# Low words and passes of weight chunks 1 and 2 moved ahead of the first main product of a linear-attention and two-layer expert kernel

## The chip, the cores and the metric

One core of a Trainium2 chip runs the whole program. The metric is the time of one execution on the device in microseconds (us), the median of several runs. The core has five engines, each with an instruction queue of its own that it works through in order: TensorE (PE in the profile, its weight loads PEld), VectorE (DVE), ScalarE (ACT), GpSimd (POOL) and SyncE (SP), which here issues the direct DMAs. Engines wait for each other through semaphores. TensorE writes into PSUM, the others read it from there.

## The reference

Three stages run one behind the other. The first is a recurrent attention over 4 batches, 8 heads, 768 steps and a head size of 48; the second a feed-forward net with a leaky rectifier; the third a choice of one of 8 experts for each of the 3072 tokens.

```python
for t in range(S):                                  # stage 1
    cur = np.einsum('bhd,bhe->bhde', u[None] * kt, vt)
    y[:, :, t] = np.einsum('bhd,bhde->bhe', rt, state + cur)
    state = wt[:, :, :, None] * state + np.einsum('bhd,bhe->bhde', kt, vt)
h = x @ w_in                                        # stage 2: 384 -> 2048 -> 384
g = np.maximum(h, 0.0) + alpha * np.minimum(h, 0.0)
x = g @ w_out
logits = xn @ en.T / tau                            # stage 3: xn, en are normed rows
expert_idx = np.argmax(logits, axis=1)
out[mask] = gate_w[mask, None] * (np.maximum(x[mask] @ w1[e], 0.0) @ w2[e])
```

The weights w_in and w_out come as 64-bit floats (the setup draws them so), and the kernel gets them as pairs of 32-bit words.

## The kernel before

**Tiles and blocks.** The 3072 tokens are 24 tiles of 128 steps (tile n is chunk n // 4 of batch n % 4), taken in 8 blocks of three. For each block the feed-forward net runs as 16 groups f of 128 hidden columns: `l1(j, f)` (L400) makes nine matmuls of 128 x 384 (high and low parts of x and of the weights in three combinations), ScalarE copies the result times alpha, VectorE takes the minimum with it, ScalarE makes the high part gh, and `l1_lo` (L421) the low part gl on VectorE. `l2(j, f)` (L425) adds nine matmuls to the block's output two groups later. In the text below the first, second and third group are f = 0, 1 and 2 of block 0.

**Weight chunks.** w_in and w_out are each cut into eight pieces of two groups. Chunk c is piece c // 2 of w_in where c is even and of w_out where it is odd. A chunk is loaded into one of four stage buffers (`load_stage`, L181) and turned into floats by `conv(q, ...)` (L190) in four steps: q = 0 scales the low words (ScalarE, L196), q = 1 merges them with the high words in two passes (VectorE, L198 and L199), q = 2 writes the rounded high part, win0h or wout0h for the first half (ScalarE, L210), q = 3 the low part (VectorE, L212). Behind q = 3 of chunk c the load of chunk c + 4 is issued on SP's queue. The chunks 0 to 3 are loaded at the start. For a w_out piece, `wprime_a` (L223) transposes it on TensorE (six transposes, two copies on ScalarE) and `wprime_b` (L237) multiplies it with the normed expert rows enT (48 small products), so that the router's logits come out of l2 as eight more columns.

**Attention pieces.** ATT (L395) lists ten pieces of a tile: 0 and 1 are scans and products on VectorE, 6 the product with r and 7 the diagonal, 2 the transposes of k into Kt, 3 the scores (TensorE, two A copies on ScalarE, masks on GpSimd), 9 the state products with their copies, 4 the output y, 5 the transposes of y into xh and xl, 8 the square of w - 0.95 on ScalarE, from which the kernel later learns whether its scaling was safe. Small PSUM results of all these pieces take turns in three buffers, those of l1 in two.

**The order.** It is written out by hand. The string PLAN (L78) is run first, item by item; each engine gets its instructions in that order. `aq.n` is piece q of tile n, `cq.c` step q of chunk c, `wk` is k warm-up matmuls, `lk.f` is l1 or l2 of group f of block 0, `pq.g` wprime_a or wprime_b of piece g, and `s` norms the expert rows (two small VectorE operations, a ScalarE product, three transposes, a copy into enT). Then a loop over steps T runs the rest (L945): for T = 0, wprime_b of piece 0, the low words of chunk 4, the passes of chunk 3, the scan of tile 3, the low part of chunk 2, gl of the first group, the high part of chunk 3; each T goes one chunk further, and group T stands at step T. What PLAN has run already the loop leaves out (`run`, L856). So the third group's l1 comes at T = 2, behind wprime_b of piece 1.

**Loads.** Tiles 0 and 1 have the two load buffers, tile 2 lies in a part of the buffer att2 (L146), from which a later weight tile is made. Tile 3's load is issued behind piece 9 of tile 0, tile 4's behind piece 9 of tile 1, those of later tiles behind piece 4. The expert rows `en` (L119) share a buffer with the wprime copies `wt` and later rows, so `s` had to come ahead of wprime_a.

Of the kernel before, what the change touches and what calls it, by code (L numbers as in the profile page):

```python
# [8 lines left out]
F32 = mybir.dt.float32  # L9
# [9 lines left out]
DM = H * D  # L19
# [3 lines left out]
NTILE = B * NCH  # L23
# [4 lines left out]
NE = 8  # L28
# [11 lines left out]
LD = LN + 3 * DM + LW  # L40
# [34 lines left out]
LAGS = [0, 1, 4, 4, 6, 7, 2]  # L75

LOADS = [(0, "w"), (0, "rk"), "id", "v", (0, "n"), "e", (1, "w"), (1, "rk"), (1, "n"), (2, "w"), (2, "rk"), (2, "n"), 0, 1, 2, 3, "u"]
PLAN = "a0.0 a1.0 a8.0 a2.0 w6 a6.0 a3.0 a7.0 w8 a0.1 a1.1 a6.1 a4.0 a3.1 a9.0 a2.1 c0.0 a7.1 w8 a0.2 a1.2 a6.2 c1.0 a4.1 w8 a3.2 a7.2 a5.0 c2.0 w6 a4.2 a5.1 a5.2 c3.0 l1.0 a8.1 a9.1 a2.2 a9.2 a8.2 c0.1 c1.1 l1.1 s c2.1 c0.2 p0.0 c3.1 c1.2 c2.2 c0.3"  # L78

AT1 = [0, 4, 8]  # L80
AT = {2: [-1, 6], 3: [-4, 1, 7]}
# [12 lines left out]
def tile_main(ctx, tc, keep, x2d, tbl, att, w_in, w_out, alpha, u_row, u_col, emb, tau, w1, w2, cst, out):  # L94
# [11 lines left out]
    rp = ctx.enter_context(tc.tile_pool(name="rows", bufs=1))  # L106
# [9 lines left out]
    u_bd = cp.tile([128, HP, 2], F32, name="u_bd")  # L116
    al_sb = cp.tile([128, KF], F32, name="al_sb")
    tau_sb = cp.tile([128, 1], F32, name="tau_sb")
    en = rp.tile([NE, DM], F32, tag="rows", name="en")  # L119
    enT = cp.tile([128, KD, NE], F32, name="enT")  # L120
    wmid = cp.tile([128, 1], F32, name="wmid")
    dev = cp.tile([128, NTILE], F32, name="dev")
# [21 lines left out]


    att2 = big.tile([128, KF // 2 * XW], F32, tag="W", name="att2")  # L146
    win = [[big.tile([128, KD, DFF // 2], F32R, tag="W", name=f"win{i}{q}") for q in "hl"] for i in range(2)]
    wout = []

# [7 lines left out]
    def load_att(n, part=None):  # L157
        if n not in ld_t:
            if n == 2:
                ld_t[n] = att2[:, 0:LD]  # L160
            else:
                ld_t[n] = ldp.tile([128, LD], F32, tag="ld", name="ld")
        m = LN + 2 * DM if n in ND else LN
        for s in {None: [slice(0, LN), slice(m, LD)] if n in ND else [slice(0, LD)], "w": [slice(LD - LW, LD)], "rk": [slice(0, LN)], "n": [slice(m, LD - LW)]}[part]:
            SP.dma_start(out=ld_t[n][:, s], in_=att[n][:, s])
# [15 lines left out]
    def load_stage(kind, g):  # L181
        t = sgp.tile([128, GF * DM, 2], I32, tag="sg", name="stg")
        if kind == "in":
            for k in range(KD):
                SP.dma_start(out=t[:, k * GF * 128:(k + 1) * GF * 128, :], in_=w_in[:, k, 2 * g * GF * 128:2 * (g + 1) * GF * 128])
        else:
            SP.dma_start(out=t, in_=w_out[:, g * GF:(g + 1) * GF, :])
        stage[kind, g] = t

    def conv(q, kind, g):  # L190

        t = stage[kind, g]
        lw, hw = t[:, :, 0], t[:, :, 1]
        lf = lw.bitcast(F32)
        if q == 0:
            ACT.activation(out=lf, in_=lw.bitcast(U32), func=AF.Copy, scale=-0.936 * 2.0 ** -51, bias=-2.0)  # L196
        elif q == 1:
            DVE.scalar_tensor_tensor(out=lw, in0=hw, scalar=3, in1=lw, op0=ALU.logical_shift_left, op1=ALU.bitwise_or)  # L198
            DVE.scalar_tensor_tensor(out=lw, in0=hw, scalar=0x3FFFFFFF, in1=lw, op0=ALU.bitwise_or, op1=ALU.bitwise_and)  # L199
        else:  # L200
            h, g0 = divmod(g, NG // 2)
            if kind == "in":
                hi, lo = (w[:, :, g0 * GW:(g0 + 1) * GW] for w in win[h])
            else:
                if h == len(wout):
                    wout_half()
                hi, lo = (w[:, g0 * GF:(g0 + 1) * GF, 0:DM] for w in wout[h])
            f3 = lf.rearrange("p (a b) -> p a b", a=(KD if kind == "in" else GF))
            if q == 2:
                ACT.activation(out=hi, in_=f3, func=AF.Copy, scale=-1.0)  # L210
            else:
                DVE.scalar_tensor_tensor(out=lo, in0=f3, scalar=-1.0, in1=hi.bitcast(F32), op0=ALU.mult, op1=ALU.subtract)  # L212
                del stage[kind, g]
# [175 lines left out]
    def warm(n):  # L389

        for _ in range(n):
            t = ps_h.tile([128, 3, 128], F32, tag="h", name="idle")
            PE.matmul(out=t, lhsT=oneb, rhs=oneb.rearrange("p (o t) -> p o t", o=1).to_broadcast([128, 3, 128]), start=True, stop=True)
# [406 lines left out]
    if True:  # L800
# [46 lines left out]
        sched = {}  # L847
        for n in range(NTILE):
            j = max(q for q in range(NB) if B0[q] <= n)
            t0 = START[n] if j == 0 else 16 * (j - 1) + (AT1 if j < 3 else AT[BLK[j]])[n - B0[j]]  # L850
            for q, d in enumerate(LAGS0 if j == 0 else LAGS1 if j == 1 else LAGS):
                sched.setdefault(t0 + d, []).append((q, n))

        ran = set()

        def run(kind, *a):  # L856
            if (kind, *a) in ran:
                return
            if kind != "w":
                ran.add((kind, *a))  # L860
            if kind == "a":
                q, n = a
                ATT[q](n)
                m = n + 3 if n < 2 else n + 2
                if q == (9 if n < 3 else 4) and n != 2 and m < NTILE:
                    load_att(m)
            elif kind == "c":
                q, c = a
                conv(q, ("in", "out")[c % 2], c // 2)
                if q == 3 and c + NSG < 2 * NG:  # L870
                    load_stage(("in", "out")[(c + NSG) % 2], (c + NSG) // 2)
            elif kind == "w":
                warm(*a)
            elif kind == "l":
                (l1, l2)[a[0] - 1](0, a[1])
            elif kind == "p":
                (wprime_a, wprime_b)[a[0]](a[1])
            else:
                DVE.tensor_scalar(out=en2, in0=en2, scalar1=1e-6, scalar2=None, op0=ALU.add)
                DVE.reciprocal(out=en2, in_=en2)  # L880
                ACT.activation(out=en, in_=en, func=AF.Copy, scale=en2)
                ep = ps_a.tile([128, KD, NE], F32, tag="a", name="ep")
                for k in range(KD):
                    PE.transpose(ep[:, k, :], en[:, k * 128:(k + 1) * 128], ident[0:NE, 0:NE])
                ACT.activation(out=enT, in_=ep, func=AF.Copy)

        def pieces(T, qs):
            for q, n in sched.get(T, []):
                if q in qs:
                    run("a", q, n)  # L890
                    if q == 6:
                        run("a", 7, n)

        def convs(T, late):
            for q, i in CONV[late]:
                c = T + OFF - i
                if 0 <= c < 2 * NG:
                    run("c", q, c)
# [43 lines left out]

        for t in PLAN.split():
            run(t[0], *(int(i) for i in t[1:].split(".") if i))
        for T in range(16 * NB + 2):  # L945
            j, f = divmod(T, 16)
            for i, d in enumerate(WPD):
                c = T + OFF - d
                if c % 2 and 0 <= c < 2 * NG:
                    run("p", i, c // 2)  # L950
            convs(T, 0)
            pieces(T, (2, 3, 4, 5))
            if 0 <= T and j < NB:
                run('l', 1, f) if j == 0 else l1(j, f)
            if T == 16 * (NB - 1):
                xg.extend(atp.tile([128, 2, ROW], F32, tag=t, name="xg") for t in ("st", "st", "at"))
                for t in xg:
                    POOL.memset(t, 0.0)
            if T >= 2:
                run('l', 2, T - 2) if T < 18 else l2((T - 2) // 16, (T - 2) % 16)  # L960
                if (T - 2) % 16 == 15:
                    o_evac((T - 2) // 16)
                    q = (T - 2) // 16
                    bg.append(chain(route(q), *((early_table(), early_loads()) if q == NB - 2 else (last_table(),) if q == NB - 1 else ())))
            if T >= 0:
                pieces(T, (0, 1, 6))
                convs(T, 2)
                if (j, f) in m_t:
                    l1_lo(j, f)
                convs(T, 1)  # L970
            step(STEP7 if j >= NB - 1 else 1)
            if T == 32:
                zero = sgp.tile([128, DM], F32, tag="sg", name="zero")
                POOL.memset(zero, 0.0)
            if 32 <= T < 32 + NTILE:
                SP.dma_start(out=out[(T - 32) * CH:(T - 31) * CH, :], in_=zero)
            for fn, i, at in EARLY:
                if T - 16 * NB == at:
                    (split, x_T)[fn](0, i)
# [31 lines left out]
        n = len(STEPS)  # L1011
# [318 lines left out]
```

## Time and profile before

| | us |
|---|---|
| median of 3 runs | 835.43 |
| lowest, highest run | 833.98, 836.77 |
| the profiled execution | 834.44 |
| its span, first to last instruction | 832.4 |
| TensorE busy | 796.8 (96% of the span) |
| VectorE busy | 585.0 (70%) |
| ScalarE busy | 436.9 (52%) |
| GpSimd busy | 297.2 (36%) |

The busy shares are means over stages with different limits. In the first 60 us attention of the first tiles, the loads and the turning of weights go on side by side, and TensorE is kept from falling silent by warm-up matmuls; behind that come the eight blocks, and behind them the experts. In the rows below, one line of a timeline gives the start in us, the time in us, the engine, the line of the kernel, the operation, what is written from what, the shape, the number of merged instructions, and in brackets the idle time before it with what ended it. One line of a window gives its start and end, its length, the busy time (and number of instructions) of PE, PEld, DVE, ACT and POOL, the granted clock of TensorE as a share of 2.4 GHz, the busy share of the DMA engines and GB/s. A line of waits says who waited for what: us in total, how often, the longest.

### The profile page before, as it was taken

To read this page: it belongs to the slowest core of one execution; us is meant where nothing else is said; L and a number is where in the kernel's file an instruction comes from. 1 tells how busy PE (TensorE), PEld (TensorE's weight loads), DVE (VectorE), ACT (ScalarE), POOL (GpSimd) and SP (SyncE) were. 2 spreads that over 40 slices of the span, in tenths; PEclk is the share of its full clock that TensorE was granted. 3 is DMA by queue.
4 is the path that set the end of the run, shared out by engine and by line. 5 is a ranking of instruction groups with operands and counts; after the bars stand their busy time and mean duration, and the time that the engine had idled before them with its cause. 6 is when DMAs were issued, how large, how long until landed. Compare 5 with 4: busy or idle time off the path is not lost. (4 is left out here: it accounts for less than half of the span.)

```text
span 832.4 us, 16488 instructions
## 1 busy us (share of the span) xinstructions
PE 796.8 (96%) x6464; PEld 758.3 (91%) x6464; DVE 585.0 (70%) x1229; ACT 436.9 (52%) x861; POOL 297.2 (36%) x365
## 2 busy tenths in 40 slices
PE   9669999999999999999999999997899999999996
PEld 5459989999999999999999999896889999999996
DVE  7478875886776676776777774646987776768662
ACT  6466664444444444544534443435556676767662
POOL 2001011343224224213214312154456777767731
PEclk9859999999999999999999999999999999999999
DMA  9434521123334323113113101046666877686750
GB/s 323 153 115 136 179 105 68 68 77 106 116 124 143 116 77 96 68 67 97 68 68 96 68 1 31 30 148 211 129 234 202 298 250 265 212 294 210 261 177 32
DMA packets 31623, 114.86 MB, mean 138 GB/s; under 512 B 5756, under 2 KB 13148, under 8 KB 29232
## 3 DMA queue, kind: packets, MB, share of 16 engines
q0 software_dynamic: 13952, 59.86, 22.1%
q1 hardware_dynamic: 17584, 53.85, 19.3%
q8 instruction: 53, 0.87, 0.5%
q14 instruction: 34, 0.28, 0.2%
HBM read 99.36 MB, written 15.51 MB: 138 GB/s over the span
## 5 line engine op out<-in xcount | busy, mean ns | idle before, releaser
L413 ACT ACTIVATE m<-h_ps,al_sb 128x384 f32<-128x384 f32 x128 | 74.1, 579 | 130.7 <-PE h_ps L409 123.6
L414 DVE TENSOR_TENSOR m<-h_ps,m 128x384 f32<-128x384 f32 x128 | 71.0, 555 | 98.6 <-ACT m L413 97.5
L417 ACT ACTIVATE gh<-m 128x384 fp32r<-128x384 f32 x128 | 67.2, 525 | 120.1 <-DVE m L414 116.8
L423 DVE TENSOR_TENSOR gl<-m,gh 128x384 fp32r<-128x384 f32 x128 | 80.3, 627 | 35.0 <-ACT gh L417 33.7
L337 POOL TENSOR_SCALAR_AFFINE_SELECT A<-A 128x512 f32<-128x512 f32 x48 | 29.8, 645 | 183.5 <-ACT A L336 183.5
L686 POOL DMA_INDIRECT raw<-in_w,wix x64 | 67.4, 1054 | 50.3 <-DVE w0l L698 23.4
L728 PE MATMUL h_ps<-yh,w0h 128*128 128x256 f32 x264 | 77.1, 292 | 3.7 <-DVE g2l L733 3.6
L728 PE MATMUL h_ps<-yl,w0h 128*128 128x256 f32 x264 | 74.7, 283 | 0.9 <-DVE yl L719 0.9
L728 PE MATMUL h_ps<-yh,w0l 128*128 128x256 f32 x264 | 74.3, 281 | 0.0
L698 DVE TENSOR_TENSOR w1l<-raw,w1h 128x768 fp32r<-128x768 f32 x64 | 60.6, 953 | 18.4 <-ACT w1h L697 12.6
L409 PE MATMUL h_ps<-xh,win0h 128*128 128x384 f32 x192 | 70.8, 369 | 2.1 <-DVE m L414 1.5
L698 DVE TENSOR_TENSOR w0l<-raw,w0h 128x768 fp32r<-128x768 f32 x64 | 60.8, 958 | 12.5 <-ACT w0h L697 11.6
L409 PE MATMUL h_ps<-xh,win1h 128*128 128x384 f32 x192 | 68.9, 359 | 0.5 <-DVE m L414 0.5
L409 PE MATMUL h_ps<-xh,win0l 128*128 128x384 f32 x192 | 66.8, 348 | 0.5 <-DVE win0l L212 0.4
L409 PE MATMUL h_ps<-xl,win0h 128*128 128x384 f32 x192 | 66.8, 348 | 0.1
L433 PE MATMUL o_ps<-wout1h,gl 128*128 128x392 f32 x192 | 65.4, 341 | 1.0 <-issue 1.0
L433 PE MATMUL o_ps<-wout0l,gh 128*128 128x392 f32 x192 | 65.5, 341 | 0.0
L433 PE MATMUL o_ps<-wout0h,gh 128*128 128x392 f32 x192 | 65.5, 341 | 0.0
L433 PE MATMUL o_ps<-wout0h,gl 128*128 128x392 f32 x192 | 65.5, 341 | 0.0
L433 PE MATMUL o_ps<-wout1h,gh 128*128 128x392 f32 x192 | 65.3, 340 | 0.1
L409 PE MATMUL h_ps<-xl,win1h 128*128 128x384 f32 x192 | 65.4, 341 | 0.0
L409 PE MATMUL h_ps<-xh,win1l 128*128 128x384 f32 x192 | 65.3, 340 | 0.0
(282 smaller groups left out, 2265.2 us busy)
## 6 DMA issues: line engine op xcount, KB each, us to landing
ld<-in_att SPq DMA_DIRECT2D x18, 1348.5 KB, 5.7
stg<-in_w_in SPq DMA_DIRECT2D x24, 256.0 KB, 3.1
stg<-in_w_out SPq DMA_DIRECT2D x8, 768.0 KB, 4.2
x2d<-rows SPq DMA_DIRECT2D x24, 194.0 KB, 7.9
out<-zero SPq DMA_DIRECT2D x24, 192.0 KB, 7.1
ld<-in_att SPq DMA_DIRECT2D x5, 512.0 KB
ld<-in_att SPq DMA_DIRECT2D x3, 452.5 KB, 5.2
raw<-in_w,wix POOLq DMA_INDIRECT x64
```

The costliest lines, as they stand in the source:

```text
L337: POOL.affine_select(out=h, in_=h, pattern=[[0, HP], [1, CH]], compare_op=ALU.is_gt, fill=0.0, base=0, channel_multiplier=-1)
L409: PE.matmul(out=h, lhsT=w[:, k, :], rhs=x[:, k, :], start=(n == 0), stop=(n == 3 * KD - 1))
L413: ACT.activation(out=m, in_=h, func=AF.Copy, scale=al_sb[:, f:f + 1])
L414: DVE.tensor_tensor(out=m, in0=h, in1=m, op=ALU.min)
L417: ACT.activation(out=gh, in_=m, func=AF.Copy)
L423: DVE.tensor_tensor(out=gl, in0=m_t.pop((j, f)), in1=gh.bitcast(F32), op=ALU.subtract)
L433: PE.matmul(out=o_t[j][i], lhsT=g[:, s], rhs=w, start=(f == 0 and n == 0), stop=(f == KF - 1 and n == 2))
L686: POOL.indirect_dma_start(out=t, out_offset=None, in_=src, in_offset=idx(wix[:, h, COL[s]:COL[s] + 1]))
L698: DVE.tensor_tensor(out=lo, in0=a, in1=hi.bitcast(F32), op=ALU.subtract)
L728: PE.matmul(out=h, lhsT=w[:, k, :], rhs=x[:, k, :], start=(n == 0), stop=(n == 3 * KD - 1))
```

## The change

PLAN gets another order; the rest are edits that make it possible.

- Piece 9 of tile 1 (state products and copies) goes from behind the first group to before the second row of warm-up matmuls; the low words of chunks 1 and 2 go to before tile 2's second scan; the passes of chunk 1 go to before tile 2's diagonal.
- Piece 5 of tile 1 goes ahead of the high part of chunk 0, and two warm-up matmuls are left out there. wprime_a of piece 0, the high part of chunk 1 and the passes of chunk 2 go ahead of the first group.
- Between the first and the second group come the low part of chunk 1 and the high part of chunk 2. Behind the second group come the low words of chunk 3, the low part of chunk 2, `s` and wprime_b of piece 0, and only then the square of tile 1, the transposes of k of tile 2 and its state products. The square of tile 2 goes to step T = 1 of the loop.
- `en` moves into a strip of att2 that tile 2 doesn't use, since wprime_a now comes ahead of `s`.
- The load of tile 4 is issued when pieces 4, 8 and 9 of tile 1 have all been run, which is now behind its square.

```diff
-PLAN = "a0.0 a1.0 a8.0 a2.0 w6 a6.0 a3.0 a7.0 w8 a0.1 a1.1 a6.1 a4.0 a3.1 a9.0 a2.1 c0.0 a7.1 w8 a0.2 a1.2 a6.2 c1.0 a4.1 w8 a3.2 a7.2 a5.0 c2.0 w6 a4.2 a5.1 a5.2 c3.0 l1.0 a8.1 a9.1 a2.2 a9.2 a8.2 c0.1 c1.1 l1.1 s c2.1 c0.2 p0.0 c3.1 c1.2 c2.2 c0.3"
+PLAN = "a0.0 a1.0 a8.0 a2.0 w6 a6.0 a3.0 a7.0 w8 a0.1 a1.1 a6.1 a4.0 a3.1 a9.0 a2.1 c0.0 a7.1 a9.1 w8 a0.2 c0.1 c0.2 a1.2 a6.2 c1.0 a4.1 w8 a3.2 c1.1 a7.2 a5.0 a5.1 c2.0 w4 a4.2 p0.0 c3.0 a5.2 c2.1 c1.2 l1.0 c3.1 c2.2 l1.1 c0.3 c3.2 s p1.0 a8.1 a2.2 a9.2"
...
-    en = rp.tile([NE, DM], F32, tag="rows", name="en")
...
     att2 = big.tile([128, KF // 2 * XW], F32, tag="W", name="att2")
+    en = att2[0:NE, LD:LD + DM]
...
+        sched[1].append((8, 2))
...
-                if q == (9 if n < 3 else 4) and n != 2 and m < NTILE:
+                if q in (4, 8, 9) and n != 2 and m < NTILE and (n > 2 or {("a", i, n) for i in (4, 8, 9)} <= ran):
                     load_att(m)
...
-                pieces(T, (0, 1, 6))
+                pieces(T, (0, 1, 6, 8))
```

## Rows read from the trace of the kernel before

**Rows 1.** The page's head: span and number of instructions.

```profile
span 832.4 us, 16488 instructions
```

**Rows 2.** Ten-microsecond windows: length, busy (count) per engine, clock, DMA share, GB/s.

```profile
20.00:30.00 10.00, 9.08 (x113) 6.34 (x113) 7.12 (x11) 4.82 (x13) 1.22 (x2) 1.00 0.53 170
30.00:40.00 10.00, 6.05 (x53) 4.80 (x52) 2.34 (x4) 5.78 (x13) 0.00 (x0) 0.84 0.56 177
40.00:50.00 10.00, 2.86 (x57) 2.34 (x57) 5.77 (x9) 6.31 (x12) 0.67 (x1) 0.50 0.24 81
50.00:60.00 10.00, 8.69 (x80) 7.70 (x80) 9.83 (x15) 5.05 (x10) 0.22 (x1) 0.64 0.33 88
```

**Rows 3.** Two long windows.

```profile
15.72:60.75 45.03, 30.71 (x348) 24.04 (x345) 29.89 (x42) 26.31 (x58) 3.33 (x6) 0.77 0.48 156
60.76:82.55 21.79, 21.59 (x256) 20.41 (x256) 19.61 (x28) 14.92 (x31) 2.71 (x5) 0.92 0.45 141
```

**Rows 4.** Timeline of VectorE, 30 to 62 us.

```profile
38.70 0.96 DVE L198 SCALAR_TENSOR_TENSOR stg<-stg 128x768 int32<-128x768 int32 x1 [5.42 <-ACT stg L196]
...
54.38 0.95 DVE L198 SCALAR_TENSOR_TENSOR stg<-stg 128x768 int32<-128x768 int32 x1
...
60.75 0.56 DVE L414 TENSOR_TENSOR m<-h_ps,m 128x384 f32<-128x384 f32 x1
```

**Rows 5.** ScalarE groups, 15.72 to 60.75: count, busy us, mean ns, idle before.

```profile
L196 ACT ACTIVATE stg<-stg 128x768 f32<-128x768 uint32 x7 | 6.3, 898 | 0.0
...
L210 ACT ACTIVATE wout0h<-stg 128x768 fp32r<-128x768 f32 x2 | 1.8, 912 | 0.9 <-DVE stg L199 0.9
...
L278 ACT ACTIVATE att<-att,wmid 128x512 f32<-128x512 f32 x1 | 0.7, 722 | 0.0
...
L234 ACT ACTIVATE wt<-wt_ps 128x512 f32<-128x512 f32 x2 | 1.2, 583 | 0.3 <-PE wt_ps L232 0.3
...
L235 ACT ACTIVATE wt<-wt_ps 128x256 f32<-128x256 f32 x2 | 0.7, 372 | 0.0
```

**Rows 6.** Timeline of ScalarE, 16 to 58 us.

```profile
19.44 1.91 ACT L307 ACTIVATE dv<-ld,dg 128x48 f32<-128x48 f32 x8
...
23.81 1.08 ACT L336 ACTIVATE A<-a_ps 128x512 f32<-128x512 f32 x2 [2.46 <-PE a_ps L333]
...
28.57 0.49 ACT L384 ACTIVATE xh<-t_ps 128x384 fp32r<-128x384 f32 x1 [0.24 <-PE t_ps L383]
...
32.11 0.58 ACT L413 ACTIVATE m<-h_ps,al_sb 128x384 f32<-128x384 f32 x1 [3.05 <-PE h_ps L409]
...
33.31 0.52 ACT L417 ACTIVATE gh<-m 128x384 fp32r<-128x384 f32 x1 [0.62 <-DVE m L414]
...
36.37 0.66 ACT L352 ACTIVATE st<-u_ps 48x192 f32<-48x192 f32 x2 [0.67 <-PE u_ps L346]
...
42.75 0.19 ACT L885 ACTIVATE enT<-ep 128x24 f32<-128x24 f32 x1 [0.57 <-PE ep L884]
```

**Rows 7.** Waits of SP's queue, first 80 us: in total, times, longest.

```profile
SPq L165 <- DMA stg<-in_w_out: 1.1, 1, 1.1
```

**Rows 8.** Timeline of TensorE at the first group.

```profile
30.57 0.44 PE L409 MATMUL h_ps<-xh,win0l 128*128 128x384 f32 x1 [0.42 <-DVE win0l L212]
```

**Rows 9.** Windows with main products alone, at either clock.

```profile
54.00:56.00 2.00, 1.95 (x6) 1.95 (x7) 1.97 (x3) 0.00 (x0) 0.00 (x0) 0.50 0.44 100
92.40:95.20 2.80, 2.80 (x17) 2.80 (x17) 0.89 (x3) 2.06 (x5) 1.22 (x2) 1.00 0.56 228
```

**Rows 10.** Window from the first group's copy to chunk 4's low words.

```profile
32.11:49.41 17.30, 7.21 (x102) 5.84 (x102) 7.00 (x11) 12.09 (x25) 0.67 (x1) 0.64 0.43 145
```

**Rows 11.** Timeline of TensorE, small groups of 44 to 63 us.

```profile
45.05 0.89 PE L243 MATMUL wq_ps<-enT,wt 128*32 128x8 f32 x48 [0.86 <-ACT wt L234]
...
58.44 0.95 PE L300 MATMUL dg_ps<-u_bd,ld 128*128 128x2 f32 x8
...
60.76 1.53 PE L232 MATMUL wt_ps<-ident,stg 128*128 128x128 f32 x6 [1.38 <-issue]
```

## The prediction

> **What bounds the kernel now.** Read the span first [rows 1]: 832.4 us, in a profiled execution of 834.44 us, 0.99 us under the median of the three runs shown (835.43). Then the windows of ten microseconds [rows 2]. Between 30 and 60 us TensorE is busy 6.05, 2.86 and 8.69 us of ten, and its granted clock falls to 0.50, the lower of its two levels (1.2 GHz). VectorE is nearly idle first (2.34 us) and full at the end (9.83 us). So the weight work that VectorE is short of time for after 50 us isn't offered to it between 30 and 40 us. Third, the two long windows [rows 3]: from 15.72 us (tile 2's first scan) to 60.75 us VectorE works 29.89 of 45.03 us, 15.1 us idle; from 60.76 to 82.55 us TensorE works 21.59 of 21.79 us. So up to 60 us the order of the work sets the time, and behind it TensorE does. Last the rows before single instructions: VectorE waits 5.42 us in front of chunk 1's first pass, because ScalarE does that chunk's low words only behind both squares of tiles 1 and 2 [rows 4].
>
> The change touches only the stretch before the third group (f = 2 of block 0). Everything behind it has the same instructions in the same order on every engine, so the gain is how much earlier the third group and the passes around it come. I follow the slower of two chains: ScalarE with VectorE, and TensorE.
>
> **Part 1: ahead of the first product.** On ScalarE tile 1's two state copies (0.66, as tile 2's in [rows 6]) and the low words of chunks 1 and 2 (2 x 0.90, [rows 5]) move ahead of tile 2's two A copies: 2.46 us. Tile 1's eight dv copies end at 21.35 us and the A copies begin at 23.81 us, after 2.46 us idle [rows 6]; the gap holds them just. What isn't hidden is TensorE: tile 1's 16 state products, estimated at 0.6 us from the 0.67 us that a state copy waits for such a group [rows 6], stand ahead of tile 2's score products, so the A copies begin near 24.4 us. The two warm-up products fewer give back about 0.4 us before tile 2's output (24.4 and all behind it keep the late 0.6; I take no gain). If the chunks' data weren't there, the cover is gone and each microsecond of waiting is one lost: the SP queue already waited out a stage transfer of w_out (1.1 us) before it issued tile 3's load, the last of this burst [rows 7], so the chunks in front of it have landed and I take 0. Bound: the DMA share of 0.53 between 20 and 30 us [rows 2] lets the burst end near 25.3 us, 2.4 us after chunk 1's low words want to start; with the second chunk 3 us at most.
>
> On VectorE chunk 1's two passes go where it sat idle in front of tile 2's dv; that costs nothing on ScalarE's chain. On TensorE and ScalarE the wprime transposes of group 0 and their copies (0.58 + 0.37 us, [rows 5]) stand ahead of tile 2's xh copy, which was at 28.57 us [rows 6]: 28.57 + 0.6 + 0.9 = 30.1 us. The first group's third product was held until 30.57 us by win0l [rows 8], which now is ready before xl is (about 31.1 us). Seven more products at 0.17 us (17 matmuls in 2.80 us at clock 1.00, [rows 9]) and the last one's end: the first group's copy begins near 32.7 us instead of 32.11 us [rows 6]. So part 1 loses 0.6 us, with 0 to 1.5 as bounds (the first group may just hide it, or the score masks on GpSimd may be held by the added passes).
>
> **Part 2: from the first group to chunk 4's low words.** Before, ScalarE needs 17.30 us from the first group's copy (32.11) to the end of chunk 4's low words (49.41), 12.09 us of it busy [rows 10]. Out of this stretch go the low words of chunks 1 and 2 (1.8), wout0h of chunk 1 (0.9), the wprime copies (0.95), tile 1's state copies (0.66) and tile 2's square with its read-out (0.9, [rows 5]): 5.2 us by durations, some 4.6 us net of the 0.1 us by which each row overlaps the next. 12.09 - 4.6 = 7.5 us busy remain. Waits that remain: twice 0.62 us for VectorE's minimum, 0.57 us for the embedding transposes, 0.67 us for tile 2's state products [rows 6], and a new one: group 0's wprime products (0.89 us at the lower clock, [rows 11]) now have nothing between enT and their copy, 1.0 us with both hand-overs. Sum 3.5 us; 11.0 us in all. Chunk 4's low words end at 32.7 + 11.0 = 43.7 us.
>
> VectorE by then has done all that comes first: chunk 2's passes at 31.1, both low parts, chunk 3's passes, tile 3's scan and products, done near 43 us. Chunk 4's first pass then starts at 43.75 us, before 54.38 us [rows 4]: 10.6 us early. From there to the third group's minimum VectorE took 6.37 us before (54.38 to 60.75). Now tile 2's square stands on ScalarE beside tile 3's, in a stretch where ScalarE (behind the scan: squares, win0h, wprime, low words, copy) ends last: +0.8 us. The minimum comes at 51.0 us, 9.8 us early.
>
> **Part 3: TensorE's chain.** The wprime copies of group 1 follow chunk 3's hi copy, near 45.5 us; its products end near 46.4 us and the third group begins. Nine matmuls at the lower clock take 2.9 us (six in 1.95 us at 0.50, [rows 9]), to 49.35. Before, the clock rose while the first l2 group ran behind it (0.50 in 54 to 56, 0.64 over 50 to 60, [rows 2, 9]); I let it rise in the same place: 4 x 0.325 + 5 x 0.17 = 2.2, to 51.5 us. Tile 3's diagonal products (0.95 us, [rows 11]) and the six wprime transposes of group 2 (about 0.85 us at full clock, half of the 1.53 us of the same rows) end at 53.3 us, before at 60.76 + 1.53 = 62.3 us: 9.0 us early. This chain is the later one, and TensorE is what the next 20 us hang on, so 9.0 us is the gain carried to the end: 834.44 - 9.0 = 825.4 us in the profiled execution, and 0.99 more by the median, 826.4 us.
>
> The moved DMAs: the stage loads behind chunks 1 and 2 go out near 34.7 and 37.3 us; tile 4's load moves behind tile 1's square and behind them on SP's queue, near 41.3 us instead of before them, and isn't read before tile 4's scan some 20 us later. Nothing waits for SP. The embedding rows in a spare strip of tile 2's buffer add no instruction.
>
> **A rule against the change.** Before, the granted clock was 0.50 from 40 to 50 us, where TensorE was busy 2.86 us [rows 2]. The Trainium skill, "TensorE: Matmul & The Clock Gate", section "What's actually happening", says that the low clock is the default and that activity releases it. By it the new order, which takes two warm-up products away and still leaves TensorE only short bursts from 34 to 45 us, has no claim to a higher clock at the third group than before; the trace agrees, 0.50 there. Rivals B and E are worked out below from [rows 2, 9].
>
> **The rivals.** A, the forecast: gain 7 to 11 us, 824 to 828.5 us.
>
> B, the clock stays low through the fourth group. Then part 3 runs 2.9 + 2.9 + 0.95 + 1.53 us from 46.4, to 54.7 us against 62.3, 7.6 us early, and the l2 group behind the fourth loses 1.4 us (half of its 2.9): 6.2 us gained, 829.2 us; with one more wait of 1.5 us 831. For it: wprime group 2 took 1.53 us before, at the lower clock. Against it: it followed a wait of 1.38 us [rows 11] on chunk 5's passes, which now are done 2 us earlier than TensorE comes to them.
>
> C, ScalarE is held by the stage data in part 1: 3 us at most, gain 6 us, 829.4 us. Against it: [rows 7].
>
> D, a larger gain: without the wait of 1.38 us TensorE keeps its full clock, and the work of 60.76 to 82.55 us, done at a mean of 0.92 [rows 3], is 0.08 x 21.79 = 1.7 us shorter. With part 1's delay hidden as well (0.6) and VectorE's lead of 0.8 us used up that is 3.1 us more, 823.3 us. Against it: later waits in this stage are VectorE's own, and it leads by no more than those 0.8 us.
>
> E, slower: the weight stage runs at the lower clock. A group pair is 18 matmuls, 5.85 us at 0.325 and 3.0 us at 0.165 [rows 9], 2.85 us lost each. If VectorE's passes break TensorE's work often enough that the clock doesn't rise from the third group on, it decides at the fourth such pair (4 x 2.85 = 11.4 over the 9.0 gained); five give 835.43 + 5.25 = 840.7 us. Against it: the granted clock of 0.92 in 60.76 to 82.55 us, with TensorE hardly waiting [rows 3].
>
> F, the change doesn't do what it says: the three small PSUM buffers, through which scores, transposes, wprime and state groups all pass in turn, hold TensorE until VectorE frees them, and the early passes push those releases back. Seven or eight waits of 1 us would be needed for no change, 835 us; the order gives each buffer its release (xl, dv, y) before its next use, and I find only one of 0.6 us.
>
> **How the numbers follow.** A 0.58, B 0.15, C 0.06, D 0.08, E 0.06, F 0.07. The time is A's, 826.4 us. The range from 822.8 (D) to 831.0 us (B with a stall, C) leaves out E, F and a little of each end, under 2 in 10. 0.3%, 2.5 us, is about what this measurement can tell from none. Faster: A to D, 0.87; within: F, 0.07; slower: E, 0.06.
>
> **What would show it.** In the profile after: A copies of tile 2 near 24.4 us behind two low-word copies without a wait; first group's copy near 32.7 us; no wait over 1.5 us on VectorE before chunk 1's passes; chunk 4's first pass near 43.8 us; the third group's products from 46.4 us; VectorE's idle time between tile 2's first scan and the third group's minimum down from 15.1 to about 6 us. The prediction is wrong if the third group comes before 60 us by less than 5 us, or if TensorE's clock in the first 25 us behind it is below 0.8.

## The result, and the profile after

| | before | after |
|---|---|---|
| median, us | 836.1 (4 runs) | 825.37 (4 runs) |
| lowest, highest | 833.98, 837.58 | 823.01, 826.17 |
| the profiled execution | 834.44 | 825.29 |
| its span | 832.4 | 823.5 |

After over before is 0.9869, with a 95% interval of 0.9838 to 0.9899. The forecast of 826.4 us is 1.0 us over the median. Between the two profiled executions the difference is 9.15 us; forecast was 9.0. The medians lie 10.7 us apart. A second comparison on another chip gave 821.85 against 831.85 us, 0.9879 (0.9864 to 0.9894), 10.0 us apart.

First the windows of the kernel after: three of the ten-microsecond ones of [rows 2], then the stretch from tile 2's first scan to the third group's minimum and the 22 us behind it.

```profile
30.00:40.00 10.00, 5.46 (x72) 4.77 (x73) 7.97 (x12) 5.61 (x13) 0.00 (x0) 0.86 0.65 216
40.00:50.00 10.00, 7.68 (x85) 6.76 (x84) 8.71 (x13) 8.25 (x19) 0.68 (x2) 0.50 0.49 143
50.00:60.00 10.00, 9.55 (x111) 8.80 (x110) 8.54 (x13) 7.23 (x15) 0.74 (x2) 0.96 0.50 158
...
15.85:50.98 35.13, 27.31 (x336) 22.41 (x333) 29.48 (x43) 26.09 (x58) 3.81 (x6) 0.81 0.63 207
50.98:73.00 22.02, 21.57 (x268) 20.29 (x266) 19.37 (x28) 14.76 (x30) 2.49 (x5) 1.00 0.40 123
```

VectorE is busy 7.97 us between 30 and 40 us, where it was 2.34 [rows 2]. In the long stretch it has the same work as before, 29.48 us against 29.89 [rows 3], in 35.13 us instead of 45.03: 5.65 us idle instead of 15.1. Not work, but waiting, has gone.

Next the timeline of VectorE after, the passes and minima that answer to [rows 4].

```profile
23.72 0.95 DVE L198 SCALAR_TENSOR_TENSOR stg<-stg 128x768 int32<-128x768 int32 x1
...
30.62 0.95 DVE L198 SCALAR_TENSOR_TENSOR stg<-stg 128x768 int32<-128x768 int32 x1
...
37.43 0.96 DVE L198 SCALAR_TENSOR_TENSOR stg<-stg 128x768 int32<-128x768 int32 x1 [0.27 <-ACT stg L196]
...
43.85 0.96 DVE L198 SCALAR_TENSOR_TENSOR stg<-stg 128x768 int32<-128x768 int32 x1 [1.12 <-ACT stg L196]
...
50.98 0.56 DVE L414 TENSOR_TENSOR m<-h_ps,m 128x384 f32<-128x384 f32 x1 [0.83 <-ACT m L413]
```

These are the first passes of chunks 1 to 4 and the third group's minimum. Chunk 1's pass comes at 23.72 us, and the wait of 5.42 us in front of it is gone; chunk 2's passes run before the first group's minimum (33.09 us). Chunk 4's first pass comes 10.5 us early (54.38 before), the third group's minimum 9.8 us early (60.75 before).

ScalarE after, where [rows 6] stand for before:

```profile
22.08 1.73 ACT L196 ACTIVATE stg<-stg 128x768 f32<-128x768 uint32 x2
24.69 0.60 ACT L336 ACTIVATE A<-a_ps 128x512 f32<-128x512 f32 x1 [0.88 <-PE a_ps L333]
...
32.48 0.58 ACT L413 ACTIVATE m<-h_ps,al_sb 128x384 f32<-128x384 f32 x1 [1.58 <-PE h_ps L409]
...
39.62 0.18 ACT L247 ACTIVATE s_wp<-wq_ps 128x16 f32<-128x16 f32 x1 [0.95 <-PE wq_ps L243]
...
42.22 0.66 ACT L352 ACTIVATE st<-u_ps 48x192 f32<-48x192 f32 x2 [0.98 <-PE u_ps L346]
42.90 0.91 ACT L196 ACTIVATE stg<-stg 128x768 f32<-128x768 uint32 x1
```

The low words of chunks 1 and 2 run in the old gap with no wait for their data (first row); chunk 4's end at 43.81 us, where before they ended at 49.41 [rows 10], and VectorE, at leisure since 42.73, takes them 0.04 us later.

TensorE after, the counterpart of [rows 11]:

```profile
45.29 0.89 PE L243 MATMUL wq_ps<-enT,wt 128*32 128x8 f32 x48 [1.63 <-ACT wt L234]
46.11 0.69 PE L409 MATMUL h_ps<-xh,win0h 128*128 128x384 f32 x1
...
50.78 0.34 PE L433 MATMUL o_ps<-wout0h,gl 128*128 128x392 f32 x1
50.96 0.34 PE L433 MATMUL o_ps<-wout0h,gh 128*128 128x392 f32 x1
...
52.30 0.94 PE L232 MATMUL wt_ps<-ident,stg 128*128 128x128 f32 x6
```

The third group starts at 46.11 us. From 50.78 us, inside the l2 group behind it, matmuls follow each other by 0.18 us: the clock has risen to its upper level (1.00 from 52 to 54 us, 0.50 from 48 to 50), and the transposes end at 53.24 us.

Last, the copies of the output of blocks 0 and 1 on VectorE. Before:

```profile
139.12 0.55 DVE L441 COPY rows<-o_ps 128x392 f32<-128x392 f32 x1
...
206.41 0.57 DVE L441 COPY rows<-o_ps 128x392 f32<-128x392 f32 x1 [0.98 <-DMA x2d<-rows]
```

After:

```profile
129.34 0.55 DVE L441 COPY rows<-o_ps 128x392 f32<-128x392 f32 x1
...
197.74 0.57 DVE L441 COPY rows<-o_ps 128x392 f32<-128x392 f32 x1 [2.10 <-DMA x2d<-rows]
```

At the end of block 0 all of VectorE's 9.78 us is there (139.12 - 129.34). At the end of block 1 it is 8.67 us, since the copy waits 2.10 instead of 0.98 us for a row buffer to be written out. In the second profile of the same kernel that wait was 1.11 us, so it isn't set by the new order.

### The profile page after: what moved, and what is told of

It is laid out like the page before. It is cut to its first block, busy times and chain, and to the rows that moved or that the text cites. A ratio compares the mean times of both kernels' runs of the same rounds, so it can differ in the third digit from the quotient of the medians.

```text
span 823.5 us, 16482 instructions
## 1 busy us (share of the span) xinstructions
PE 791.7 (96%) x6462; PEld 753.9 (92%) x6462; DVE 584.3 (71%) x1229; ACT 436.4 (53%) x861; POOL 297.3 (36%) x365
## 5 line engine op out<-in xcount | busy, mean ns | idle before, releaser
L698 DVE TENSOR_TENSOR w0l<-raw,w0h 128x768 fp32r<-128x768 f32 x64 | 60.7, 958 | 12.2 <-ACT w0h L697 11.3
L433 PE MATMUL o_ps<-wout1l,gh 128*128 128x392 f32 x192 | 65.4, 340 | 0.0
```

The lines of the kernel that those rows point to most:

```text
L433: PE.matmul(out=o_t[j][i], lhsT=g[:, s], rhs=w, start=(f == 0 and n == 0), stop=(f == KF - 1 and n == 2))
L698: DVE.tensor_tensor(out=lo, in0=a, in1=hi.bitcast(F32), op=ALU.subtract)
```

## The experiments

What could be behind the gain: the *passes theory* (weight passes reach VectorE in its idle time), the *pieces theory* (squares and state pieces stood in ScalarE's way behind the first group), the *clock theory* (TensorE's clock at the third group), the *TensorE theory* (my part 3: TensorE's chain ends last), and later the *buffer theory* (the three small PSUM buffers). Each comparison has its own runs of the kernel before on the same chip: 835.44 us for the first four kernels, 831.85 for the next three, 832.4 for the last. Profiles differ ahead of the stretch, too: tile 2's first scan starts between 15.64 and 15.91 us in ten of the twelve, but at 16.36 in the second profile of the kernel after and at 16.41 in the first of "chunk 3 early too". So where one of these two is compared with another profile, times below are counted from that scan or say so.

### Only the pieces

Order of the kernel before, with squares, Kt and state pieces behind the second group, at the end of PLAN (tile 2's square at T = 1).

```diff
-l1.0 a8.1 a9.1 a2.2 a9.2 a8.2 c0.1 c1.1 l1.1 s ... c2.2 c0.3
+l1.0 c0.1 c1.1 l1.1 s ... c2.2 c0.3 a8.1 a9.1 a2.2 a9.2
```

> The order of before, but the squares and state pieces of tiles 1 and 2 behind the second group (tile 2's square at T = 1); the weight work isn't moved ahead of the first group. Passes theory (mine): what counts is VectorE's weight passes in its early idle time, so this alone gives about a third: chunk 4's first pass near 50.3 us, the third group's minimum near 57.4 us (60.75 before, 50.98 after), time 3 to 4 us under before. Pieces theory (rival): the squares and state pieces in ScalarE's queue ahead of chunk 1's low words were the cost; then this alone gives nearly everything, minimum near 52 us, time 8 us or more under before. Clock theory (rival): gain as far as the third and fourth group run at 1.0.

Measured: 832.92 us, ratio 0.9973 (0.9957 to 0.9989). VectorE's timeline in this kernel:

```profile
34.58 0.96 DVE L198 SCALAR_TENSOR_TENSOR stg<-stg 128x768 int32<-128x768 int32 x1 [1.35 <-ACT stg L196]
...
57.42 0.56 DVE L414 TENSOR_TENSOR m<-h_ps,m 128x384 f32<-128x384 f32 x1 [0.82 <-ACT m L413]
```

The wait of 5.42 us falls to 1.35, but the third group's minimum comes only 3.3 us early. The pieces account for a third of the lead at most.

### Only the weights

Order of the kernel after, with the pieces back behind the first group.

```diff
-a7.1 a9.1 w8 ... l1.0 c3.1 c2.2 l1.1 c0.3 c3.2 s p1.0 a8.1 a2.2 a9.2
+a7.1 w8 ... l1.0 a8.1 a9.1 a2.2 a9.2 a8.2 c3.1 c2.2 l1.1 c0.3 c3.2 s p1.0
```

> The order of after, but squares and state pieces of tiles 1 and 2 all back behind the first group; only the weight work stands early. Passes theory: chunk 3's low words come near 41.7 us instead of 37.4, chunk 4's first pass near 47.0 us, the third group's minimum near 53.3 us, time about 7 us under before and 2 to 2.5 us over after. Pieces theory: most of the gain is gone, minimum near 59 us, time 2 us under before at most.

Measured: 827.45 us, ratio 0.9911 (0.9893 to 0.9929). VectorE:

```profile
39.32 0.56 DVE L414 TENSOR_TENSOR m<-h_ps,m 128x384 f32<-128x384 f32 x1 [5.43 <-ACT m L413]
...
52.84 0.56 DVE L414 TENSOR_TENSOR m<-h_ps,m 128x384 f32<-128x384 f32 x1
```

VectorE still waits 5.43 us, now before the second group's minimum, and yet the third is 7.9 us early: the passes were done before. So the early weights carry most of the gain and the pieces the rest (3.3 + 7.9 is more than 9.8, so 1.4 us can be had by either). As a main cause the pieces theory falls.

### The clock in the kernel before

Warm-up products alone: six ahead of `s`, fourteen ahead of step T = 1.

```diff
-c1.1 l1.1 s
+c1.1 l1.1 w6 s
...
+            if T == 1: warm(14)
```

> The order of before with 20 warm-up products added in TensorE's idle time (6 behind the second group, 14 ahead of the wprime transposes of piece 1), nothing else. Clock theory: the gain is the clock; the third and fourth group at full clock give 3 to 5 us of the 9. Passes theory: VectorE has no gap between 48.3 and 69 us, so the faster products wait for it: third group's minimum within 0.5 us of 60.75, time within 1.5 us of before.

Measured: 835.78 us, ratio 1.0013 (1.0003 to 1.0024). Windows of this kernel:

```profile
54.00:56.00 2.00, 1.96 (x11) 1.96 (x12) 1.97 (x3) 0.00 (x0) 0.00 (x0) 1.00 0.41 122
56.00:58.00 2.00, 1.92 (x15) 1.83 (x13) 2.00 (x3) 0.50 (x1) 0.00 (x0) 1.00 0.78 267
58.00:60.00 2.00, 0.00 (x0) 0.00 (x0) 1.97 (x4) 1.97 (x6) 0.23 (x1) 0.97 0.37 72
60.00:62.00 2.00, 1.25 (x7) 1.28 (x7) 1.87 (x4) 1.38 (x5) 0.00 (x0) 0.50 0.91 331
```

The clock is at its upper level from 54 us (0.50 before, [rows 9]), and TensorE only gets earlier to a wait for VectorE, silent from 58 to 60 us; then the clock is 0.50 again. The third minimum stands at 60.72 us (60.75 before). The clock theory falls for the kernel before.

### The clock in the kernel after

Warm-up products in the kernel after, so that its third group runs at the upper level.

```diff
-c3.2 s p1.0 a8.1 a2.2 a9.2
+c3.2 w10 s p1.0 a8.1 a2.2 w5 a9.2
...
+            if T == 2: warm(12)
```

> The order of after with 27 warm-up products in TensorE's idle time between the second and the third group (10 behind the second group, 5 ahead of tile 2's state products, 12 at T = 2), nothing else. My step that TensorE's chain is the later one: the third group's products are 1.5 us shorter, the l2 group behind them 0.6, the wprime transposes of piece 2 start as soon as chunk 5's passes end (50.2 us) instead of 52.3; the third group's minimum stays at 51 us (ScalarE), the fifth group's comes up to 1.5 us earlier, time 0.5 to 1.5 us under after. If VectorE's chain is the one that counts behind the third group, no more than 0.3 us under after. If the warm-up products hold tile 2's state products up, up to 1 us over.

Measured: 826.8 us, ratio 0.9899 (0.9882 to 0.9915); the kernel after had 0.9869 (0.9838 to 0.9899). The clock is 1.00 in every window from 44 to 58 us. TensorE in this kernel:

```profile
50.46 0.75 PE L232 MATMUL wt_ps<-ident,stg 128*128 128x128 f32 x4
...
55.68 0.49 PE L333 MATMUL a_ps<-ld 64*128 64x128 f32 x2
58.16 0.60 PE L333 MATMUL a_ps<-ld 64*128 64x128 f32 x6 [2.00 <-ACT s_wp L247]
```

And two of its windows behind that:

```profile
56.00:58.00 2.00, 0.16 (x2) 0.00 (x0) 2.00 (x5) 1.29 (x3) 0.00 (x0) 1.00 0.70 255
...
60.00:62.00 2.00, 2.00 (x8) 2.00 (x7) 0.00 (x0) 0.70 (x2) 1.22 (x2) 0.50 0.60 245
```

The transposes start 1.8 us earlier (52.30 after). But tile 3's second group of scores needs a small PSUM buffer that ScalarE frees only when it copies wprime's products: TensorE waits 2.00 us, is busy 0.16 us between 56 and 58, and from 60 us the clock is 0.50. The nine products of the fifth group start no later than after, but take 2.9 us (59.25 to 62.19) instead of 1.7 (59.47 to 61.15), and ScalarE waits 1.73 us for them. The fifth group's minimum stands at 63.04 us (61.97 in the first profile after), block 0's copy at 130.95 (129.34).

The 0.5 to 1.5 us that the TensorE theory asked for don't come: the lead of 1.8 us ends in a wait for ScalarE, and the lower clock behind that wait costs more than a microsecond. The run is no clean test, though. Five of the warm-up products stand ahead of tile 2's state products, for which ScalarE waits 1.83 us (0.98 after), and the third group's minimum comes 0.5 us later behind the scan (35.6 us, 35.1 after). The fourth stands at 40.5 us in both, since VectorE doesn't wait here for tile 3's diagonal products, as it does in the kernel after (0.55 us, see part 3 below): there the earlier TensorE was worth half a microsecond.

The Trainium skill, "TensorE: Matmul & The Clock Gate", section "What's actually happening", says that the low clock is the default and activity releases it. Both kernels with added warm-up products agree with it, 1.00 behind the warm-up products and 0.50 behind a silence; neither gained time by it.

### The norm of the expert rows earlier

VectorE's and ScalarE's part of `s` (written n) to a place before the second warm-up row, its transposes and the copy to enT behind a9.1.

```diff
-a6.1 a4.0 ... a9.1 w8 ... c3.2 s p1.0
+a6.1 n a4.0 ... a9.1 s w7 ... c3.2 p1.0
```

> The order of after with the norming of the expert rows taken apart: VectorE's two small operations and ScalarE's product go ahead of tile 0's output, the transposes and their copy behind tile 1's state products (one warm-up product fewer there). ScalarE's chain behind the second group loses the product, the copy and two waits for TensorE, 2.3 us. Passes theory: VectorE then is the one that comes last, chunk 4's first pass at 42.5 us (43.85 in after), the third group's minimum near 49.6 us (50.98), time 1 to 1.5 us under after. TensorE theory (the step of the prediction by which its chain is the later one): the wprime transposes of piece 2 come as they did but for 0.5 us, time within 0.5 us of after.

Measured: 822.65 us, ratio 0.9884 (0.9869 to 0.9899), beside 0.9879 for the kernel after. Counted from tile 2's first scan (15.75 us here, 16.36 in the kernel after beside it), chunk 4's first pass comes at 26.9 us (28.0 after), the third minimum at 34.0 (35.1), the fifth at 46.1 (46.5, and 46.1 in the first profile after). TensorE:

```profile
56.70 0.49 PE L333 MATMUL a_ps<-ld 64*128 64x128 f32 x4 [1.70 <-ACT s_wp L247]
```

A window behind that, and ScalarE's copy of the fifth group:

```profile
58.00:60.00 2.00, 2.00 (x8) 1.84 (x7) 0.42 (x1) 1.30 (x3) 1.11 (x2) 0.50 0.73 292
```

```profile
61.20 0.58 ACT L413 ACTIVATE m<-h_ps,al_sb 128x384 f32<-128x384 f32 x1 [1.89 <-PE h_ps L409]
```

The front gains 1.1 us, as the passes theory said; the time doesn't. TensorE waits 1.70 us for the same small buffer, and even so its second scores start 1.6 us earlier than in the first profile after (40.95 us behind the scan, 42.54 after). But behind that wait the clock is 0.50, and the nine products of the fifth group take 2.8 us (58.16 to 60.99) instead of 1.7. ScalarE waits for them, 0 to 0.4 us of the lead is left at the fifth minimum, and the time shows no difference.

### Chunk 3 early too

The kernel above, with chunk 3's low words ahead of the first group, its passes ahead of the second minimum, and tile 2's square at T = 3.

```diff
-c2.1 c1.2 l1.0 c3.1 c2.2 l1.1 c0.3 c3.2 p1.0
+c2.1 c1.2 c0.3 l1.0 c3.1 c2.2 c1.3 l1.1 c3.2 p1.0
...
-        sched[1].append((8, 2))
+        sched[3] = sched.get(3, []) + [(8, 2)]
```

> As e5_norm_early, and the low words of chunk 3 ahead of the first group's copy, its passes ahead of the second group's minimum, tile 2's square at T = 3 instead of T = 1. Passes theory: VectorE's waits of 0.99, 0.27 and 1.12 us between 34 and 44 us go as well, chunk 4's first pass near 41.2 us, the third group's minimum near 47.8 us, block 0's copy out 2.5 to 3.2 us ahead of after, time 2 to 3 us under after. TensorE theory: the third group at the lower clock and what stands behind it hold the gain to 1 us.

Measured: 820.3 us, ratio 0.9858 (0.9843 to 0.9874); run again 820.18, 0.986 (0.9843 to 0.9878). In the first profile chunk 4's first pass comes at 42.18 us, the third minimum at 48.62, the fifth at 60.89, block 0's copy at 128.26, 2.2 us before the kernel after beside it (130.50); both stand late from tile 2's first scan on. In the profile of the second run, which doesn't, they come at 41.19 (41.2 expected), 47.62 (47.8), 59.22 and 126.64. TensorE in the first:

```profile
57.29 1.16 PE L333 MATMUL a_ps<-ld 64*128 64x128 f32 x14 [1.18 <-ACT s_wp L247]
```

The clock stays at 1.00 behind this shorter wait (56 to 60 us). It is the lowest time of all, 1.6 us under the kernel after beside it; but the two intervals overlap, so better than after is likely and not shown.

### Only chunk 1 early

The kernel after, with the low words and passes of chunk 2 back behind the second group.

```diff
-c0.1 c0.2 a1.2 ... c2.1 c1.2 l1.0 c3.1 c2.2 l1.1 c0.3 c3.2 s
+c0.1 a1.2 ... c2.1 l1.0 c3.1 l1.1 c0.2 c1.2 c2.2 c0.3 c3.2 s
```

> The order of after, but chunk 2's low words and passes stay behind the second group; only chunk 1's go ahead. Passes theory: VectorE's two passes (1.87 us) and ScalarE's low words (0.9 us) come back into the chain, chunk 4's first pass near 45.9 us, the third group's minimum near 53.0 us, time 2 us over after. Rival (one chunk fills the idle time already): minimum within 0.5 us of 50.98, time within 0.5 us of after.

Measured: 825.83 us, ratio 0.9933 (0.9919 to 0.9948). ScalarE and VectorE in this kernel:

```profile
35.78 0.86 ACT L196 ACTIVATE stg<-stg 128x768 f32<-128x768 uint32 x1
38.66 0.89 ACT L210 ACTIVATE win0h<-stg 128x768 fp32r<-128x768 f32 x1 [2.02 <-DVE stg L199]
```

```profile
36.67 0.96 DVE L198 SCALAR_TENSOR_TENSOR stg<-stg 128x768 int32<-128x768 int32 x1 [1.35 <-ACT stg L196]
...
47.37 0.96 DVE L198 SCALAR_TENSOR_TENSOR stg<-stg 128x768 int32<-128x768 int32 x1 [1.37 <-ACT stg L196]
```

The third minimum comes at 54.55 us, 38.6 us behind tile 2's first scan and so 3.5 us later than in the kernel after (35.1); expected were 53.0, 2.0 us later. A miss in size, and it teaches something: I had counted chunk 2's steps as work, but they hand over from one engine to the other, low words, two passes, high part, and behind the second group nothing lies between them. ScalarE waits 2.02 us and VectorE 1.35, each for the other. Done early, the same steps lie between other work and the waits vanish.

### Scores ahead of wprime's products

The best kernel, with the Kt transposes and scores of tiles 3 to 5 ahead of wprime_b at T = 4, 8 and 12, so that they take their buffer before wprime does, and tile 2's square at T = 5.

```diff
+            if T in (4, 8, 12):
+                pieces(T, (2, 3))
```

> As e6_chunk3_early, with two places changed: at T = 4, 8 and 12 the transposes of k and the scores of that step's tile go ahead of wprime_b, so that the second score group no longer needs the small PSUM buffer that wprime_b's products hold until ScalarE copies them, and tile 2's square goes from T = 3 to T = 5. Buffer theory (rival F's mechanism, as the next limit): TensorE's wait of 1.18 us in front of the second score group at 56 us is gone, the fifth group's minimum comes near 60.0 us instead of 60.9 (ScalarE ends last then), block 0's copy out 0.9 us ahead of e6, time 0.5 to 1 us under it. VectorE theory (its passes alone pace the stage): the fifth group's minimum within 0.3 us of 60.9, time as e6.

Measured: 821.69 us, ratio 0.9869 (0.9851 to 0.9887). Here and in the best kernel run beside it the wait at the scores was looked for in TensorE's waits from 50 to 76 us. Scores first:

```profile
PE t_ps L383 <- ACT dg L304: 1.2, 1, 1.2
PE wq_ps L243 <- ACT Kt L324: 0.8, 1, 0.8
PE dg_ps L300 <- ACT s_wp L247: 0.5, 1, 0.5
PE wt_ps L232 <- DVE y L369: 0.2, 1, 0.2
```

The best kernel:

```profile
PE a_ps L333 <- ACT s_wp L247: 1.2, 1, 1.2
PE t_ps L383 <- ACT dg L304: 0.8, 1, 0.8
PE wt_ps L232 <- ACT st L352: 0.6, 1, 0.6
```

The wait in front of the scores is gone, and others make up for it, 2.7 us in all against 2.6: wprime's products now wait for Kt, the diagonal products for wprime's copy, and the transposes of y longer for dg. Between 70 and 82 us the clock is 0.72 here, 1.00 in the best kernel. Its fifth minimum comes at 59.77 us (59.22 beside it), its seventh at 72.71 (71.43). The buffer theory is right about that wait and wrong about the time: the three buffers pass on what isn't waited for here. That the time is 1.5 us over the best kernel beside it isn't shown, since the two intervals overlap.

## Why the prediction was right

**What bounds the stretch.** The order does: the same VectorE work in 9.9 us less. Right, and shown by the two halves of the change, 3.3 and 7.9 us at the third minimum.

**Part 1**, 0.6 us lost. The A copies came at 24.69 us (24.4 forecast): the wait for the score products, 0.88 us, was larger than the 0.6 estimated. By the first group's copy (32.48, forecast 32.7; before 32.11) 0.4 us of it was left. Rival C falls: no wait for stage data.

**Part 2**, 11.0 us from the first group's copy to chunk 4's low words. It was 11.3: the new wait for wprime's products 0.95 (1.0 taken), for the state products 0.98 (0.67 taken). Chunk 4's first pass 43.85 (43.75), third minimum 50.98 (51.0). The stage loads went out at 34.66 and 36.99 us (34.7, 37.3), tile 4's at 40.78 (41.3).

**Part 3**, TensorE. Third group 46.11 (46.4), clock rising in the l2 group as assumed, transposes ending at 53.24 (53.3), so 9.0 us early as said. Rival B falls with that. The step by which this chain is the later one holds for the next group. Tile 3's diagonal products stand on TensorE at 51.49 us, 7.0 us early (58.44 before, [rows 11]), and VectorE, which is 9.8 us early, now waits for them. Its product dv and the fourth group's minimum before:

```profile
61.97 0.56 DVE L309 TENSOR_TENSOR dv<-ld,dg 128x384 f32<-128x384 f32 x1
...
65.65 0.55 DVE L414 TENSOR_TENSOR m<-h_ps,m 128x384 f32<-128x384 f32 x1
```

After:

```profile
52.69 0.56 DVE L309 TENSOR_TENSOR dv<-ld,dg 128x384 f32<-128x384 f32 x1 [0.55 <-ACT dg L304]
...
56.36 0.55 DVE L414 TENSOR_TENSOR m<-h_ps,m 128x384 f32<-128x384 f32 x1
```

The fourth minimum comes 9.3 us early, the fifth too (71.28 before, 61.97 after). What failed is that this smaller lead is carried to the end, and that it is all TensorE's: at the end of block 0 it is 9.78 us again. The 0.5 us come back between the seventh minimum (lead 9.34) and the thirteenth (9.77). There the clock of the kernel before falls to 0.57 twice (84 to 88 and 108 to 112 us), and that of the kernel after stays at 1.00; that this is the reason is likely, and no run tests it.

The 9.15 us of the profiled pair is close to the 9.0 forecast in part by luck: the lead of 9.78 us loses 1.12 us in the longer wait at block 1's copy, which the second profile doesn't have, and 8.67 us is left there, 8.9 in the span. The medians' 10.7 and 10.0 us are more than either. The intervals of both comparisons, 8.4 to 13.5 and 8.8 to 11.3 us, hold 9.0 and 9.8 alike.

**Rivals D, E and F.** TensorE ran the 22 us behind the third minimum at a clock of 1.00 (0.92 before, [rows 3]). D would have had 1.7 us from that; from the third minimum to block 0's copy it is 78.4 us in both (50.98 to 129.34, 60.75 to 139.12) and 79.0 in the second profile after (51.49 to 130.50), where the clock is 0.59 from 76 to 80 us and 0.60 from 100 to 104. So the higher clock gave no more than the 0.5 us that the wait for the diagonal products took. E's lower clock didn't come with the change in that stretch, but its mechanism shows in two experiments: behind a wait of 1.70 or 2.00 us the fifth group runs at 0.50 and takes more than a microsecond longer. F was the nearest to a real limit: TensorE in the kernel after waits only 0.4 us for the scores' buffer, but where the front comes 1.1 us earlier still, it waits 1.70 us there, and with the lower clock behind it next to nothing is left at the fifth group.

**Open.** Whether the best kernel beats the one after, what sets the pace from the fourth group to the end of block 0, and what share of the front's last 2 us is lost at the row buffers of block 1, where VectorE waits 0.98 to 3.21 us for a write in eleven of the twelve profiles.

## What to carry to other kernels

In a prologue that runs on in-order queues, look for an engine that is idle first and full later, and ask which instruction of another engine's queue holds back what it is given: here two low-word copies and the passes they release, moved into gaps, carried most of ten microseconds. Follow both chains to one marker that both kernels have (here a minimum of the same group), and check the claim that one of them is the later by making that one faster alone. Count from an instruction ahead of the change: two profiles of the same kernel here differ by 0.5 us before the stretch begins. Look at the granted clock behind every new wait of TensorE: here a wait of 1.70 us cost nothing by itself, and the lower clock behind it took the microsecond that was gained. A chunk's steps that alternate between two engines cost their hand-overs wherever nothing else lies between them, so spread them out rather than counting their work.

## What was not expected of the hardware

GpSimd's score masks of tile 2 took 1.70 us, beginning beside chunk 1's second pass, against 1.22 before. The kernel before:

```profile
24.47 1.22 POOL L337 TENSOR_SCALAR_AFFINE_SELECT A<-A 128x512 f32<-128x512 f32 x2 [6.28 <-ACT A L336]
```

The kernel after:

```profile
25.36 1.70 POOL L337 TENSOR_SCALAR_AFFINE_SELECT A<-A 128x512 f32<-128x512 f32 x2 [7.03 <-ACT A L336]
```

In the kernel before it was VectorE that paid: the product dv that began 0.61 us behind the masks took 1.02 us, against 0.63 after. In the kernel after the pass that ran when the masks began kept its 0.96 us. The Trainium skill, "SBUF — State Buffer", section "Who interferes with whom", says that a VectorE instruction with two SBUF inputs contends with a GpSimd one that reads SBUF, and that who issues first decides who is held; both traces agree that they meet: the product grew by 0.4 us in the one (1.02 - 0.63), the masks by 0.5 in the other (1.70 - 1.22). That only one of the two grows is not so: in the kernel before, tile 0's masks begin at 12.29 us and take 1.72 us, and the product of two SBUF tiles that begins behind them, at 12.58, takes 0.94. In the second profile of the kernel after the product begins first (12.64, the masks at 12.94) and takes 0.69, the masks 1.48. Over the twelve profiles the product takes 0.94 to 1.15 us in the ten where the masks begin first, and 0.69 in the two where it does, so who starts first goes with VectorE's share of the price. The spans on GpSimd are rough, and no run here takes a meeting alone away.
